# A gated linear-attention and mixture-of-experts kernel: the decayed k of the state update from untransposed k and a decay table that passes through DRAM

## The chip, the cores and the metric

The kernel runs on one core of one Trainium2 chip. The metric is device microseconds of one execution: the median of several. Engine names are those of the profile: PE (matrix engine; PEld its weight loads), DVE (vector), ACT (scalar), POOL, and SP, whose queue issues most DMAs.

## What is computed

```python
def _attn_ref(q, k, v, alpha):                    # (4, 8, 768, 48) each
    state = zeros((B, H, D, D))
    for t in range(S):
        state = alpha[:, :, t, :, None] * state + einsum('bhd,bhe->bhde', k[:, :, t], v[:, :, t])
        y[:, :, t] = einsum('bhd,bhde->bhe', q[:, :, t], state)

def _moe_ref(x, w_gate, w1, w2):                  # x (3072, 384), 8 experts, hidden 1024
    P = exp(logits - max);  8 rounds of row and column normalisation
    for e in range(E):
        out += P[:, e:e + 1] * (maximum(x @ w1[e], 0) @ w2[e])
```

The change touches the attention's state alone: over 128 tokens it is multiplied by the product of their alphas, and k^T v is added, each k times the alphas of the tokens behind it in these 128.

## The kernel before, in words

**Chunks and groups.** A batch element's 768 tokens are six chunks of 128. Two chunks make a group of 256 tokens, named batch_group: 0_0 to 3_2, twelve in all. The first four chunks (0_0 and 0_1) take a path of their own (`direct_chunk`) that the change leaves as it is. The other ten groups pass through `attn_block`, `attn_decays` and, for each chunk, `attn_chunk` with `attn_tail`.

**A group's block.** `attn_block` loads q, k and alpha with 16 tokens in a partition's row: 128 partitions are 16 sub-blocks of 8 heads. POOL and DVE multiply scores inside each 16 tokens (tile `AB`) and fold the alphas into q and k, so that `al[:, 0]` ends as the product of a sub-block's 16 alphas. The last step hands everything over through DRAM, all on SP's queue: `ks`, `qs`, `ds` (that product) and `As` are written and read back with tokens in the partitions as `KN`, `QN`, `DN`, `an`, and `VN` is loaded from v. The loads of the next block (`qt`, `al`, `kt`) stand behind it, on SP's queue or, for two groups, on POOL's.

**Decays.** `attn_decays` turns `DN` on PE (`psd`), and DVE and ACT build small tables from it (`pre`, `suf`, `q32`, `k32`, `q128`, `k128`, `dtot`): products of the sub-blocks' decays before or behind a sub-block.

**A chunk.** `attn_chunk` turns k and q on PE (`psk`, `psq`; copies `Tk`, `Tq`), makes decayed copies (`decq`, `deck`), multiplies scores (`psl`), and then multiplies `Tk` in place by `k128` on POOL. `attn_tail` computes y in `psy` from the old state `ST` and the scores `A`, turns the decayed k back with four PE transposes into `pskn`, copies it to `kb` on ACT, and multiplies `kb` with `VN` into `pss`, from which `ST` is updated. The last chunk of a batch element has no update: 16 of these 20 chunks turn k back. The chunk's y then goes, scaled, to `xT` (two f16 halves), the gate product `psg` reads it, and the experts read it later.

**What sets the order.** The two strings `START` and `UNIT` are an order written out by hand: `bN` is a step of block N, `cN` of chunk N, `dN` the decays of group N, `wN` a step of loading expert N's weights, `f` 0.45 us of expert matmuls (`moe_tile`; tiles `ps`, `h`, `r`). Each engine runs its instructions strictly in that order. The expert matmuls evacuate PSUM through four banks: in the first layer ACT writes the high half of `h` and DVE the low half, and a bank is free after DVE; in the second layer ACT alone copies to `r`. An expert's `w1` is loaded by eight DMAs into tile `xT` (`load_expert`), squared and summed by ACT (tile `w1m`), and PE multiplies the sums with `ones` into `pst_w`.

Of the kernel before, what the change touches and what calls it, by code (L numbers as in the profile page):

```python
# [9 lines left out]
F32 = mybir.dt.float32  # L10
# [15 lines left out]
def tile_gla_moe(ctx: ExitStack, tc: tile.TileContext, q, k, v, alpha, wg, w1, w2, out):  # L26
    nc = tc.nc
    B, H, S, D = q.shape
    NT, DM = out.shape
    E, _, FF = w1.shape  # L30
    P = 128
    U = 256
    NU = S // U
    NCH = U // P
# [3 lines left out]
    NP = H // 2  # L38
# [263 lines left out]
    for x in PRE + SUF + Q32 + K32:  # L302
        GE.memset(x, 1.0)

    ids = iter(range(1 << 20))
    hp1 = early.enter_context(tc.tile_pool(name="hp1", bufs=1, side="right"))
    fst = ExitStack()
# [24 lines left out]
    def load_v(x, b, t0, Q=SP):  # L332
        for r in range(2):
            Q.dma_start(x[:, :, r * DP:r * DP + D], v[b].rearrange("(j r) t d -> r t j d", r=2)[r, t0:t0 + P])
# [144 lines left out]
    def attn_block(b, u, got):  # L479

        g = b * NU + u
        t0 = u * U
        nm = f"{b}_{u}"
        vec = VE
        src = lambda x: x[b, :, t0:t0 + U].rearrange("h (n t) d -> n h (t d)", t=16)
        qt, kt, al = (ap1.tile([P, 16, D], F32, tag=x, name=f"{x}_{nm}") for x in ("qt", "kt", "al"))
        for x, y in ((qt, q), (al, alpha), (kt, k)):
            (GE if lop[0] else SP).dma_start(x, src(y))
        yield
        A = AB[g % 2]  # L490
        Af = A.rearrange("p s t -> p (s t)")
        pool = GE
        qd = qt

        def mult(eng, tag, shape, o, x, y):
            t = ap1.tile([P, *shape, D], F32, tag=tag, name=f"{tag}_{nm}_{next(ids)}")
            eng.tensor_mul(t, x, y)
            return o, t

        def total(o, t):  # L500
            vec.tensor_reduce(o, t, axis=AX.X, op=ALU.add)

        def level(L):

            nb = 8 // L
            Q = qd.rearrange("p (n z t) d -> p n z t d", z=2, t=L)
            K = kt.rearrange("p (n z t) d -> p n z t d", z=2, t=L)

            Dl = al.rearrange("p (n z t) d -> p n z t d", z=2, t=L)

            def cut(n, s, w):
                return ([w, L], A[:, n * 2 * L + s:n * 2 * L + s + w, n * 2 * L + L:(n + 1) * 2 * L],
                        Q[:, n, 1:2].to_broadcast([P, w, L, D]),
                        K[:, n, 0, s:s + w].unsqueeze(2).to_broadcast([P, w, L, D]))

            if L == 1:
                todo = [(pool, "tmp1", [8], Af[:, 1:256:34], Q[:, :, 1, 0], K[:, :, 0, 0])]
            elif L == 2:
                o = [bass.AP(tensor=Af.tensor, offset=Af.offset + s * 16 + 2, ap=[Af.ap[0], [68, 4], [1, 2]])
                     for s in range(2)]  # L520
                todo = [(pool, f"tmp{s + 1}", [4, 2], o[s], Q[:, :, 1],
                         K[:, :, 0, s:s + 1].to_broadcast([P, 4, 2, D])) for s in (1, 0)]
            elif L == 4:
                todo = [(pool, "tmp4", *cut(n, 0, 4)) for n in (1, 0)]
            else:
                todo = [(vec, "tmp8", *cut(0, 4, 4))] + [(pool, "tmp4", *cut(0, s, 2)) for s in (0, 2)]

            def merge(ko=kt, qo=qd):
                z = lambda x, i: x.rearrange("p (n z t) d -> p n z t d", z=2, t=L)[:, :, i]
                pool.tensor_mul(z(ko, 0), K[:, :, 0], Dl[:, :, 1, 0:1].to_broadcast([P, nb, L, D]))  # L530
                eng = pool if g in (2, 3) else vec
                eng.tensor_mul(z(qo, 1), Q[:, :, 1], Dl[:, :, 0, 0:1].to_broadcast([P, nb, L, D]))
                eng.tensor_mul(Dl[:, :, 0, 0], Dl[:, :, 0, 0], Dl[:, :, 1, 0])
            return todo, merge

        ko, qo = kt, qd
        if True:

            t = mult(pool, "tmp4", [16], Af[:, 0:256:17], qt, kt)
            yield  # L540
            total(*t)
            yield
            vec.tensor_mul(qt, qt, al)
            for L in (1, 2, 4, 8):
                todo, merge = level(L)
                for x in todo:
                    t = mult(pool if lop[0] else x[0], *x[1:])
                    yield
                    total(*t)
                    if L == 8:  # L550
                        yield
                merge()
            yield
        dma = SP.dma_start
        qs = dr.tile([H, U, D], F32, tag="qs", name=f"qs_{nm}")
        ks = dr.tile([H, U, D], F32, tag="ks", name=f"ks_{nm}")
        ds = dr.tile([H, 16, D], F32, tag="ds", name=f"ds_{nm}")
        As = dr.tile([H, U, 16], F32, tag="As", name=f"As_{nm}")
        qn, kn, dn = QN[g % 2], KN[g % 2], DN[g % 2]
        vn = VN[g % 2]  # L560
        an = ap2.tile([P, NCH, H, 16], F32, tag="an", name=f"an_{nm}")
        def put(t, t_):
            for x, y in ((ks, ko), (qs, qo)):
                dma(x[:, t:t_].rearrange("h (n t) d -> n h (t d)", t=16), y[t // 2:t_ // 2])

        put(0, U)
        dma(ds.rearrange("h n d -> n h d"), al[:, 0])
        if True:
            dma(As.rearrange("h (n s) t -> n h (s t)", s=16), Af)
        for c in range(NCH):  # L570
            sl = slice(c * P, (c + 1) * P)
            dma(kn[:, c, :, :D], ks[:, sl].rearrange("h t d -> t h d"))
            dma(qn[:, c, :, :D], qs[:, sl].rearrange("h t d -> t h d"))
            if c == 0:
                dma(dn[:, :, :D], ds.rearrange("h n d -> n h d"))
            dma(an[:, c], As[:, sl].rearrange("h p t -> p h t"))
            load_v(vn[:, c], b, t0 + c * P)
        got.update(qn=qn, kn=kn, dn=dn, vn=vn, an=an)
        yield

    def attn_decays(b, u, got):

        nm = f"{b}_{u}"
# [14 lines left out]
        e4 = ap2.tile([P, NCH, NP, 2], F32, tag="e4", name=f"e4_{nm}")  # L598
        dtot = ap2.tile([P, NCH, NP], F32, tag="dtot", name=f"dtot_{nm}")
        q128 = ap2.tile([P, NCH, NP, 2, 4], F32, tag="q128", name=f"q128_{nm}")  # L600
        k128 = ap2.tile([P, NCH, NP, 2, 4], F32, tag="k128", name=f"k128_{nm}")
        mul(x3(e2), d_[:, :, 0:4:2], d_[:, :, 1:4:2])
        cpy(x3(q32)[:, :, 1], d_[:, :, 2])
        cpy(x3(k32)[:, :, 0], d_[:, :, 1])
# [8 lines left out]
        cj = lambda x: x.rearrange("p c j z n -> p (c j) z n")  # L613
        e4b = lambda z: e4.rearrange("p c j z -> p (c j) z")[:, :, z:z + 1].to_broadcast([P, NCH * NP, 4])
        mul(cj(q128)[:, :, 1], cj(pre)[:, :, 1], e4b(0))
        mul(cj(k128)[:, :, 0], cj(suf)[:, :, 0], e4b(1))
        cpy(cj(q128)[:, :, 0], cj(pre)[:, :, 0])
        cpy(cj(k128)[:, :, 1], cj(suf)[:, :, 1])
        got.update(pre=pre, suf=suf, q32=q32, k32=k32, q128=q128, k128=k128, dtot=dtot)

    def attn_chunk(b, ch, got):

# [2 lines left out]
        first, last = ch == 0, ch == S // P - 1  # L625
        tt = b * (S // P) + ch
        nm = f"{b}_{ch}"
        T2 = []
        for s in "kq":
            ps = psa.tile([P, 512], F32, tag="psa", name=f"ps{s}_{nm}")  # L630
# [17 lines left out]
        def decayed_all(x, eng, tab):  # L648
            xi = x.rearrange("p j (n t) -> p (j n) t", t=16)
            eng.tensor_mul(xi, xi, tab.rearrange("p j z b -> p (j z b)").unsqueeze(2).to_broadcast([P, NP * 8, 16]))  # L650
# [30 lines left out]
        if not first:  # L681
            decayed_all(QT, VE, got["q128"][:, c])
        if not last:
            decayed_all(KT, GE, got["k128"][:, c])
        yield
        K_, Q_ = ([x[:, j] for j in range(NP)] for x in (KT, QT))
        yield from attn_tail(b, ch, vn[:, c], K_, Q_, A, got["dtot"][:, c])

    def attn_tail(b, ch, vn, KT, QT, A, dtot):

        first, last = ch == 0, ch == S // P - 1
        tt = b * (S // P) + ch
# [18 lines left out]
        y = psy[:, :DM]  # L711
        ab = ap2.tile([P, DM], BF16, tag="ab", bufs=1, name=f"ab_{nm}")
        SE.activation(ab, y, AF.Abs, scale=2.0 ** -10)
        if not last:
            psk = psa.tile([P, 512], F32, tag="psa", name=f"pskn_{nm}")
            for j in range(NP):
                tr(psk[:, j * P:(j + 1) * P], KT[j], ident)
            kb = ap2.tile([P, NP, P], F32, tag="kb", bufs=1, name=f"kb_{nm}")
            SE.copy(kb.rearrange("p j t -> p (j t)"), psk)
        yield  # L720
        psn = psy[:, DM:]
        for i in range(KT_):
# [10 lines left out]
        if not last:  # L733
            pss = psa.tile([P, 512], F32, tag="psa", name=f"pss_{nm}")
            for j in range(NP):
                for r in range(2):
                    pr = slice(r * DP, r * DP + D)
                    mm(pss[pr, j * D:(j + 1) * D], kb[:, j, pr], vn[:, j, pr])
            pv = pss[:, :NP * D].rearrange("p (j e) -> p j e", j=NP)
            for r in range(2):  # L740
                pr, cr = slice(r * DP, r * DP + D), slice(r * D, (r + 1) * D)
                if first:
                    SE.copy(Sn[pr, :, cr], pv[pr])
                else:
                    GE.tensor_mul(Sn[pr, :, cr], So[pr, :, cr],
                                         dtot[pr].unsqueeze(2).to_broadcast([D, NP, D]))
                    VE.tensor_add(Sn[pr, :, cr], Sn[pr, :, cr], pv[pr])
# [720 lines left out]
```

## Time and profile before

| | |
|---|---|
| median of 3 runs | 1655.09 us (1653.46 to 1657.01) |
| profiled execution, device time | 1656.76 us |
| its span, first to last instruction | 1655.1 us |
| PE busy | 1605.3 us, 97% |
| DVE, ACT, POOL busy | 1266.7, 933.0, 394.0 us |
| granted PE clock, mean | 0.987 of full |
| chain that ended last, PE's share | 86% |

The device time of the profiled execution is 1.7 us above its span. Rows of the trace give the start in us from the span's start, then the duration; `x16` behind a shape counts instructions merged into the row; brackets give the idle time before it and what ended it.

### The profile page before, as it was taken

How to read it: one execution, taken by the hardware profiler on the slowest of the kernel's cores; microseconds unless marked ns; L12 is line 12 of the kernel's file. 1: busy time of each engine (PE TensorE's matmuls, PEld its weight loads, DVE VectorE, ACT ScalarE, POOL GpSimd, SP SyncE). 2: the span in 40 equal slices, each digit the busy share in tenths (PEclk: the TensorE clock that was granted, in tenths of full speed). 3: DMA queues.
4: the chain of work that ended last, by engine and by line, in shares of the span. 5: the costliest groups of instructions: out<-in, count | busy, mean ns of one | idle time of the engine just before them, and what ended most of it. 6: DMA issues, size and time to landing. Idle time of an engine off the chain costs nothing.

```text
span 1655.1 us, 53978 instructions
## 1 busy us (share of the span) xinstructions
PE 1605.3 (97%) x23260; PEld 1429.1 (86%) x23260; DVE 1266.7 (77%) x2852; ACT 933.0 (56%) x2250; POOL 394.0 (24%) x395
## 2 busy tenths in 40 slices
PE   5689999999999999999999999999999999999998
PEld 4567777777777777777999999999999999999998
DVE  5877766665666574367798978898888888899998
ACT  4655543334333334355777767666766676666554
POOL 5447544643644462165000000000000000000000
PEclk9789999999999999999999999999999999999999
DMA  7463244144134313130312131213121312123332
GB/s 164 103 142 92 59 105 96 34 109 105 53 72 105 84 46 76 38 84 30 102 54 88 59 97 59 97 53 94 53 94 59 97 59 88 61 67 116 116 117 87
DMA packets 173903, 137.15 MB, mean 83 GB/s; under 512 B 109120, under 2 KB 163648, under 8 KB 173664
## 3 DMA queue, kind: packets, MB, share of 16 engines
q1 hardware_dynamic: 171920, 127.01, 28.0%
q0 software_dynamic: 1744, 6.70, 1.6%
q8 instruction: 182, 2.98, 0.7%
q14 instruction: 57, 0.47, 0.1%
HBM read 86.50 MB, written 47.17 MB: 81 GB/s over the span
## 4 chain that ended last, share of the span: by engine, by line
PE 86%; DVE 7%; ACT 3%; issue 2%; DMA 1%; SPq 0%; POOL 0%; DVEq 0%; ACTq 0%; POOLq 0%
PE ps L67 33%; PE p1a L67 13%; PE p2x L67 12%; PE p2y L67 6%; PE p1c L67 6%; PE p1d L67 4%; PE p2v L67 3%; PE psl L67 2%; PE psy L67 2%; DVE h L58 1%; DVE acc L58 1%; DVE hf L58 1%; DVE T L58 1%; ACT w L58 1%; DVE w L58 1%
## 5 line engine op out<-in xcount | busy, mean ns | idle before, releaser
L67 PEld LDWEIGHTS <-h 128*128 128x128 f16 x6684 | 570.3, 98 | 103.1 <-DVE h L58 0.8
L67 PEld LDWEIGHTS <-w 128*128 128x128 f16 x8424 | 602.3, 98 | 39.3 <-issue 6.6
L58 DVE TENSOR_TENSOR h<-hf,h 128x256 f16<-128x256 f32 x472 | 286.0, 616 | 34.3 <-ACT h L58 33.0
L67 PE MATMUL ps<-xT,w 128*128 128x256 f16 (+1 forms) x2664 | 302.3, 274 | 5.3 <-DVE h L58 3.2
L67 PE MATMUL ps<-w,h 128*128 128x384 f16 x1728 | 299.1, 327 | 0.2 <-DVE w L58 0.2
L67 PE MATMUL p2x<-w,h 128*128 128x192 f16 x2820 | 271.0, 246 | 0.0
L58 ACT CAST h<-hf 128x256 f16<-128x256 f32 x472 | 248.9, 570 | 13.1 <-DVE hf L58 8.2
L58 DVE TENSOR_TENSOR hf<-hf 128x256 f32<-128x256 f32 x354 | 181.6, 513 | 44.8 <-ACT hf L58 36.3
L58 DVE SCALAR_TENSOR_TENSOR h<-ps,h 128x256 f16<-128x256 f32 (+1 forms) x296 | 118.4, 413 | 115.3 <-ACT h L58 114.1
L58 ACT ACTIVATE h<-ps 128x256 f16<-128x256 f32 (+1 forms) x296 | 110.6, 376 | 161.7 <-PE ps L67 161.3
L58 POOL TENSOR_TENSOR tmp<-qt,kt 128x768 f32<-128x768 f32 (+2 forms) x87 | 156.8, 1808 | 133.9 <-DVE qt L58 84.3
L67 PE MATMUL p1a<-xT,w 128*128 128x128 f16 x2160 | 179.5, 219 | 0.0
L67 PE MATMUL p1c<-xT,w 128*128 128x128 f16 x2160 | 159.9, 219 | 0.0
L67 PEld LDWEIGHTS <-wx 128*128 128x128 f16 x2160 | 147.3, 98 | 7.2 <-issue 6.5
L58 ACT ACTIVATE hf<-p1d 128x256 f32<-128x256 f32 x118 | 45.1, 382 | 184.4 <-DVE h L58 157.7
L67 PE MATMUL p2y<-w,h 128*128 128x192 f16 x1404 | 135.0, 246 | 0.0
L67 PE MATMUL p1a<-xc,wx 128*128 128x128 f16 x1440 | 119.6, 219 | 4.7 <-ACT v L58 2.0
L58 DVE TENSOR_REDUCE AB<-tmp 128x16 f32<-128x768 f32 (+2 forms) x90 | 81.3, 903 | 53.0 <-POOL tmp L58 52.7
L58 ACT COPY r<-ps 128x384 f32<-128x384 f32 x72 | 34.2, 476 | 99.3 <-PE ps L67 60.2
L58 ACT COPY A<-psl 16x128 f32<-16x128 f32 (+3 forms) x164 | 52.4, 326 | 48.2 <-PE psl L67 46.6
L67 PE MATMUL p1d<-xT,wx 128*128 128x128 f16 x720 | 79.5, 219 | 0.0
L67 PE MATMUL p1a<-xc,w 128*128 128x128 f16 x720 | 79.5, 219 | 0.0
(237 smaller groups left out, 2020.3 us busy)
## 6 DMA issues: line engine op xcount, KB each, us to landing
accd<-acc SPq DMA_DIRECT2D x48, 384.0 KB, 2.6
acc<-accd SPq DMA_DIRECT2D x48, 384.0 KB, 3.2
raw<-r SPq DMA_DIRECT2D x72, 192.0 KB, 1.9
ri<-raw SPq DMA_DIRECT2D x72, 192.0 KB, 2.9
w1f<-in_moe_w_dram SPq DMA_DIRECT2D x20, 384.0 KB, 6.8
w2f<-in_moe_w_dram SPq DMA_DIRECT2D x5, 1536.0 KB, 6.9
VN<-in_v_dram SPq DMA_DIRECT2D x48, 96.0 KB, 2.9
out_dram<-acc SPq DMA_DIRECT2D x11, 384.0 KB, 4.0
```

What stands on the lines that cost most here:

```text
L58: r = f(*a, **k_)
L67: tc.keep_in_program_order(nc.tensor.matmul(out_, lhsT, rhs, start=start, stop=stop, **k_))
```

## The change

A second handover is added to the first. Every group's `al[:, 0]` is also written to a DRAM array `dsw` with 15 places for each head and chunk: eight are the chunk's sub-blocks, and the seven behind them hold ones, written once into each of two such arrays. Two DMAs read it as `win`: each partition is a sub-block and a head and gets the seven places behind its own. In `attn_decays` four DVE products reduce the seven to one decay (`win[:, 0]`), which goes to DRAM as `td` (16 sub-blocks by 384) and is read, sub-block by sub-block with 16 tokens each, as the tile `kb` at the start of `attn_chunk`. POOL multiplies `kb` by the untransposed `kn`, at the place where it multiplied `Tk`. The four transposes, the `pskn` bank, the ACT copy and the table `k128` go; `kb` has two buffers in place of one. `win` shares the buffer `tmp2` of the block.

```diff
+    dsw = [dr.tile([H, NCH, 15, D], F32, tag=f"dsw{i}", bufs=1, name=f"dsw{i}") for i in range(2)]
...
     def attn_block(b, u, got):
...
+        if g < ND // NCH + 2:
+            SP.dma_start(dsw[g % 2][:, :, 8:].rearrange("h c n d -> (h c) n d"),
+                         ones[:2 * H, None, :D].to_broadcast([2 * H, 7, D]))
...
         dma(ds.rearrange("h n d -> n h d"), al[:, 0])
+        for c in range(NCH):
+            dma(dsw[g % 2][:, c, :8].rearrange("h n d -> n h d"), al[c * 64:c * 64 + 64, 0])
...
             load_v(vn[:, c], b, t0 + c * P)
+        win = ap1.tile([P, 7, D], F32, tag="tmp2", name=f"win_{nm}")
+        for c in range(NCH):
+            e = dsw[g % 2][0, c, 1]
+            dma(win[c * 64:c * 64 + 64], bass.AP(tensor=e.tensor, offset=e.offset,
+                                                 ap=[[D, 8], [NCH * 15 * D, H], [1, 7 * D]]))
...
     def attn_decays(b, u, got):
...
         mul(cj(q128)[:, :, 1], cj(pre)[:, :, 1], e4b(0))
-        mul(cj(k128)[:, :, 0], cj(suf)[:, :, 0], e4b(1))
         cpy(cj(q128)[:, :, 0], cj(pre)[:, :, 0])
-        cpy(cj(k128)[:, :, 1], cj(suf)[:, :, 1])
+        win = got["win"]
+        mul(win[:, 0:3], win[:, 0:3], win[:, 3:6])
+        mul(win[:, 0], win[:, 0], win[:, 6])
+        mul(win[:, 1], win[:, 1], win[:, 2])
+        mul(win[:, 0], win[:, 0], win[:, 1])
+        td = dr.tile([NCH * 8, DM], F32, tag="td", name=f"td_{nm}")
+        SP.dma_start(td.rearrange("n (h d) -> n h d", h=H), win[:, 0])
+        tab = []
+        for c in range(NCH):
+            e = td[c * 8]
+            tab.append(bass.AP(tensor=e.tensor, offset=e.offset, ap=[[DM, 8], [0, 16], [1, DM]]))
...
     def attn_chunk(b, ch, got):
...
+        kb = None
+        if not last:
+            kb = ap2.tile([P, H, D], F32, tag="kb", name=f"kb_{nm}")
+            SP.dma_start(kb, got["tab"][c])
...
         if not last:
-            decayed_all(KT, GE, got["k128"][:, c])
+            GE.tensor_mul(kb, got["kn"][:, c, :, :D], kb)
...
-        if not last:
+        if not last and kb is None:
             psk = psa.tile([P, 512], F32, tag="psa", name=f"pskn_{nm}")
             for j in range(NP):
                 tr(psk[:, j * P:(j + 1) * P], KT[j], ident)
-            kb = ap2.tile([P, NP, P], F32, tag="kb", bufs=1, name=f"kb_{nm}")
-            SE.copy(kb.rearrange("p j t -> p (j t)"), psk)
+            kb = ap2.tile([P, H, D], F32, tag="kb", name=f"kb_{nm}")
+            SE.copy(kb, psk.rearrange("p (h d) -> p h d", h=H)[:, :, :D])
```

SP's queue in group 0_2, the first that goes through `attn_block`; `xT` are the weights of expert 2. Before:

```order
L58 DMA an_2_1939<-As_2_1938 128x8x16
L58 DMA VN_123<-in_v_dram 128x4x48 x2
L58 DMA KN_118<-ks_2_1936 128x8x48
L58 DMA QN_116<-qs_2_1935 128x8x48
L58 DMA an_2_1939<-As_2_1938 128x8x16
L58 DMA VN_123<-in_v_dram 128x4x48 x2
L58 DMA xT_1_80<-in_moe_w_dram 32x3x512 x4
L58 DMA xT_1_83<-in_moe_w_dram 32x3x512 x4
L58 DMA xT_2_81<-in_moe_w_dram 128x4x384
```

The same place after:

```order
L58 DMA KN_118<-ks_2_1939 128x8x48
L58 DMA QN_116<-qs_2_1938 128x8x48
L58 DMA an_2_1942<-As_2_1941 128x8x16
L58 DMA VN_123<-in_v_dram 128x4x48 x2
L58 DMA win_2_1960<-dsw_148 64x1x336 x2
L58 DMA dsw_149<-ones 16x7x48
L58 DMA td_2_2000<-win_2_1960 128x48
L58 DMA kb_4_2003<-td_2_2000 128x1x384
L58 DMA xT_1_80<-in_moe_w_dram 32x3x512 x4
L58 DMA xT_1_83<-in_moe_w_dram 32x3x512 x4
```

Five DMAs now stand between the last `VN` load and the weights, among them `td`, which reads what DVE has written, and `kb`, which reads what `td` has written.

DVE's queue at the decays of group 1_2, as in all later groups; `xT` here is the low half of a chunk's output, which `psg` on PE reads. Before:

```order
L58 TENSOR_TENSOR dtot_2_4609<-e_1_2_4608 128x8
L58 TENSOR_TENSOR q_1_2_4610<-pre_130,e_1_2_4608 128x8x4
L58 TENSOR_TENSOR k_1_2_4611<-suf_132,e_1_2_4608 128x8x4
L58 TENSOR_TENSOR xT_1_83<-ys_3_4538,xT_1_80 128x3x128
L58 TENSOR_TENSOR decq_1_4_4671<-Tq_4_4669,q_1_134 128x256
L58 TENSOR_TENSOR deck_1_4_4673<-Tk_4_4662,k_1_136 128x256
```

The same place after:

```order
L58 TENSOR_TENSOR dtot_2_4617<-e_1_2_4616 128x8
L58 TENSOR_TENSOR q_1_2_4618<-pre_130,e_1_2_4616 128x8x4
L58 TENSOR_TENSOR win_2_4599<-win_2_4599 128x144
L58 TENSOR_TENSOR win_2_4599<-win_2_4599 128x48 x3
L58 TENSOR_TENSOR xT_1_83<-ys_3_4541,xT_1_80 128x3x128
L58 TENSOR_TENSOR decq_1_4_4684<-Tq_4_4682,q_1_134 128x256
```

The one table product is replaced by the four products on `win`, whose first needs both `win` DMAs landed. On PE the 16 rows of four transposes into `pskn` are gone and nothing else has moved; on POOL each product on `Tk` is replaced in place by one on `kb`.

## Rows read from the trace of the kernel before

**Rows 1.** Windows: length; busy PE, PEld, DVE, ACT, POOL; clock; DMA share; GB/s.

```profile
120.00:160.00 40.00, 37.68 (x474) 28.59 (x473) 30.09 (x59) 23.70 (x54) 26.29 (x22) 1.00 0.33 93
200.00:300.00 100.00, 99.79 (x1309) 76.45 (x1308) 68.70 (x132) 38.85 (x109) 46.85 (x39) 1.00 0.38 91
```

**Rows 2.** The tile `pskn`: duration min/median/max ns, first and last start.

```profile
L70 PE MATMUL pskn<-ident,Tk x64: 272/273/330, 145.7 to 679.5; 128*128 128x128 f32 x64
```

**Rows 3.** Timeline of PE: the transposes of one chunk and what follows.

```profile
223.22 0.66 PE L70 MATMUL pskn<-ident,Tk 128*128 128x128 f32 x4
223.72 2.11 PE L67 MATMUL ps<-w,h 128*128 128x384 f16 x12
```

**Rows 4.** The chain that ended last, in group 0_2.

```profile
113.01 4.32 DMA VN<-in_v_dram
...
117.80 6.60 DMA xT<-in_moe_w_dram
...
124.91 3.40 ACT w L58 x8
...
128.36 0.39 PE pst_w L67 x2
```

**Rows 5.** Timeline of SP's queue in group 0_2.

```profile
112.26 1.20 SPq L58 DMA_DIRECT2D VN<-in_v_dram  x2
113.51 14.62 SPq L58 DMA_DIRECT2D xT<-in_moe_w_dram  x10
```

**Rows 6.** Timeline of DVE in group 0_2: the table product.

```profile
114.57 0.19 DVE L58 TENSOR_TENSOR k<-suf,e 128x32 f32<-128x32 f32 x1
```

**Rows 7.** The tile `ds`: writing and reading 24 KB, 20 DMAs.

```profile
DMA to landing us min/median/max: 2.1/3.4/5.0
```

**Rows 8.** Windows of 4 us around group 0_2.

```profile
104.00:108.00 4.00, 2.04 (x131) 1.74 (x127) 3.11 (x13) 0.68 (x3) 0.17 (x1) 0.97 1.09 280
...
116.00:120.00 4.00, 4.00 (x69) 3.18 (x68) 3.27 (x4) 1.19 (x3) 3.23 (x3) 0.75 1.03 212
```

**Rows 9.** Timeline of DVE in group 1_0.

```profile
169.55 0.19 DVE L58 TENSOR_TENSOR k<-suf,e 128x32 f32<-128x32 f32 x1
170.78 0.52 DVE L58 TENSOR_TENSOR decq<-Tq,q 128x256 f32<-128x256 f32 x1 [1.04 <-ACT Tq L58]
171.22 2.11 DVE L58 TENSOR_TENSOR deck<-Tk,k 128x256 f32<-128x256 f32 x1
173.26 2.02 DVE L58 TENSOR_TENSOR decq<-Tq,pre 128x256 f32<-128x256 f32 x1
...
177.87 0.74 DVE L58 SCALAR_TENSOR_TENSOR h<-ps,h 128x256 f16<-128x256 f32 x2
```

**Rows 10.** Timeline of POOL beside it.

```profile
170.97 2.08 POOL L58 TENSOR_TENSOR A<-an,mask 128x1024 f32<-128x1024 f32 x1
```

**Rows 11.** Timeline of DVE, the next chunk's `deck`.

```profile
188.03 0.84 DVE L58 TENSOR_TENSOR deck<-Tk,k 128x256 f32<-128x256 f32 x1
```

**Rows 12.** Timeline of SP's queue in group 1_0.

```profile
167.18 5.29 SPq L58 DMA_DIRECT2D VN<-in_v_dram  x2
```

**Rows 13.** Timeline of PE in group 1_0: first-layer matmuls, nine a bank.

```profile
173.48 2.13 PE L67 MATMUL ps<-xT,w 128*128 128x256 f16 x18
...
177.21 3.12 PE L67 MATMUL ps<-xT,w 128*128 128x256 f16 x27
```

**Rows 14.** Timeline of DVE in group 1_2.

```profile
286.25 0.18 DVE L58 TENSOR_TENSOR k<-suf,e 128x32 f32<-128x32 f32 x1
286.92 0.56 DVE L58 TENSOR_TENSOR xT<-ys,xT 128x384 f16<-128x384 f32 x1 [0.49 <-ACT xT L58]
290.70 0.51 DVE L58 TENSOR_TENSOR decq<-Tq,q 128x256 f32<-128x256 f32 x1 [3.22 <-ACT Tq L58]
```

**Rows 15.** Timeline of PE in group 1_2: the gate product.

```profile
290.81 0.29 PE L67 MATMUL psg<-wg,xT 128*128 128x18 f16 x6
```

**Rows 16.** Timeline of SP's queue in group 1_2.

```profile
283.30 1.38 SPq L58 DMA_DIRECT2D VN<-in_v_dram  x2
```

More of the change, by code (lines that the diff above doesn't have):

```diff
@@ L577, in attn_block @@
             load_v(vn[:, c], b, t0 + c * P)
+        win = ap1.tile([P, 7, D], F32, tag="tmp2", name=f"win_{nm}")
[3 more added lines that the diff above has]
+                                                 ap=[[D, 8], [NCH * 15 * D, H], [1, 7 * D]]))
+        got["win"] = win
         got.update(qn=qn, kn=kn, dn=dn, vn=vn, an=an)
@@ L600, in attn_decays @@
         q128 = ap2.tile([P, NCH, NP, 2, 4], F32, tag="q128", name=f"q128_{nm}")
-        k128 = ap2.tile([P, NCH, NP, 2, 4], F32, tag="k128", name=f"k128_{nm}")
         mul(x3(e2), d_[:, :, 0:4:2], d_[:, :, 1:4:2])
@@ L615, in attn_decays @@
         mul(cj(q128)[:, :, 1], cj(pre)[:, :, 1], e4b(0))
-        mul(cj(k128)[:, :, 0], cj(suf)[:, :, 0], e4b(1))
         cpy(cj(q128)[:, :, 0], cj(pre)[:, :, 0])
-        cpy(cj(k128)[:, :, 1], cj(suf)[:, :, 1])
-        got.update(pre=pre, suf=suf, q32=q32, k32=k32, q128=q128, k128=k128, dtot=dtot)
+        win = got["win"]
[9 more added lines that the diff above has]
+            tab.append(bass.AP(tensor=e.tensor, offset=e.offset, ap=[[DM, 8], [0, 16], [1, DM]]))
+        got.update(pre=pre, suf=suf, q32=q32, k32=k32, q128=q128, tab=tab, dtot=dtot)
     def attn_chunk(b, ch, got):
@@ L683, in attn_chunk, with attn_tail @@
         if not last:
-            decayed_all(KT, GE, got["k128"][:, c])
+            GE.tensor_mul(kb, got["kn"][:, c, :, :D], kb)
         yield
         K_, Q_ = ([x[:, j] for j in range(NP)] for x in (KT, QT))
-        yield from attn_tail(b, ch, vn[:, c], K_, Q_, A, got["dtot"][:, c])
-    def attn_tail(b, ch, vn, KT, QT, A, dtot):
+        yield from attn_tail(b, ch, vn[:, c], K_, Q_, A, got["dtot"][:, c], kb)
+    def attn_tail(b, ch, vn, KT, QT, A, dtot, kb=None):
         first, last = ch == 0, ch == S // P - 1
@@ L737, in attn_tail @@
                     pr = slice(r * DP, r * DP + D)
-                    mm(pss[pr, j * D:(j + 1) * D], kb[:, j, pr], vn[:, j, pr])
+                    mm(pss[pr, j * D:(j + 1) * D], kb[:, 2 * j + r, :D], vn[:, j, pr])
             pv = pss[:, :NP * D].rearrange("p (j e) -> p j e", j=NP)
```

## The prediction

> **What bounds the kernel now.** I read the busy time by stage first. The reader is to see PE there: 99.79 us busy of 100 from 200 to 300 us, 37.68 of 40 from 120 to 160 [rows 1]. Once the expert matmuls run without a break PE is the bound, so a PE instruction taken out there is time won in full, and a stall put in there is time lost in full. Then the view of the tile `pskn`: 64 transposes, the first at 145.7 us, the last at 679.5, all in that stretch [rows 2]. Last, the chain that ended last, because the first group of the new path runs before PE is saturated: in group 0_2 it goes through a `VN` load that lands at 113.01 + 4.32 = 117.33, a weight load `xT` that lands at 117.80 + 6.60 = 124.40, ACT's squares of these weights, and `pst_w` on PE at 128.36 [rows 4]. So SP's queue at 113.5 is on the path that sets the end, and that is where the change puts five more DMAs.
>
> **What it removes.** The price of a transpose is not its duration of 273 ns, since matmuls overlap. It is the step from the start of the four to the start of the next matmul: 223.72 - 223.22 = 0.50 us [rows 3]; the two other chunks that I read gave 0.49. 16 chunks x 0.495 = **7.9 us won**. The ACT copy and the table product `k128` that go too are worth nothing: they lie beside a saturated PE and PE does not wait for them. POOL's product on `kb` stands where the one on `Tk` stood, with 384 columns in place of 512; nothing either. The `pss` matmuls keep their shape.
>
> **What it adds, group 0_2.** SP ends the last `VN` issue at 113.46 (112.26 + 1.20) and began the weights at 113.51 [rows 5]. Now two `win` DMAs come between. They queue behind `VN`, which lands at 117.33 [rows 4], and bring 172 KB: I take 118.5, with 117.3 and 119.5 as ends. DVE, which did the table product at 114.57 [rows 6], waits for them; its four products, each hardly more than the 0.19 of that one and in part dependent, take about 0.8 (estimate), to 119.3. `td` waits for DVE and `kb` for the landing of `td`; two such transfers are in the rows of `ds`, 2.1 to 5.0 us, median 3.4 [rows 7]. I take 2.4, near the lowest, because the queue is empty then: 121.7. With 0.6 for the issue of `kb` the weights start at 122.3, not at 113.51. Before, the eighth weight load landed 10.9 us after the first issue, behind a full queue. Now eight issues at 0.6 (`VN` took 1.20 for two) and one landing of 3.4 give 8.2: 130.5 in place of 124.40. ACT's four squares took 3.40 [rows 4]; two of them can run while the other four loads land, so 1.75 are left: 132.3, against 128.31. PE waits at `pst_w` **4.0 us longer**. Ends: 1.6 (`win` together with `VN`, 2.1 for `td`, loads in 7.4) and 8.4 (119.5, 5.0, 9.1). DVE's own delay here ends before that and is covered by the same wait of PE.
>
> **PE's clock in that wait.** From 104 to 108 PE was busy 2.04 of 4 us; from 116 to 120, busy throughout, its mean granted clock was still 0.75 [rows 8]: it had fallen from 2.4 to 1.2 GHz in between and came back in that slice, which cost 1.0 us of it. A wait of five us at 128 is a deeper hole than that of 104. I take 1.0 to 2.0, **1.5 us lost**; ends 0 (the clock stays) and 5 (ten us at half clock).
>
> **Group 1_0.** SP ends the last `VN` issue at 172.47 (167.18 + 5.29) [rows 12]: the `win` issues, 0.6 each, end at 173.6 and land at about 176.1 (2.5 after). DVE wanted to pass at 169.55 and began `decq` at 170.78 [rows 9]. Now it begins at 176.9, 6.1 late. It gets some of this back: `deck` and the second `decq` took 2.11 and 2.02 beside POOL's `A` and what follows it on POOL [rows 9, 10], but 0.84 [rows 11] and 0.52 [rows 9] without; POOL is done before 176.9, so 2.8 come back and the low half of `h` is 3.3 late. PE needs it: the five first-layer tiles start at 173.48 (two) and 177.21 (three, 1.0 apart) [rows 13], there are four banks, and the fifth, at 179.25, takes the bank that DVE freed at 178.25 (177.87 and one product) [rows 9]. 3.3 late against a slack of 1.0: **2.4 us lost**. Ends: 1.5 (`win` in 2.1 after the first issue) and 6.0 (nothing regained, landing in 3.4).
>
> The Trainium skill ("SBUF — State Buffer", section "SBUF: two separate sides") says that VectorE and GpSimd share one port pair by an exclusive lock, held for the whole instruction, so that the other one waits. Rows 9 to 11 agree with it: 2.11 beside a POOL instruction of 2.08, 0.84 without. By it the delayed DVE work runs free of POOL; if contention followed it instead, this group would lose 2.8 more and the kernel come out at 1659.2.
>
> **The other eight groups.** In 1_2 SP ends `VN` at 284.68 [rows 16]; the two `dsw` issues push that by about 0.5 (most of their 1.2 falls into waits for landings), the second `win` starts at 285.8 and lands at 288.8 (3.0, between 2.1 and 3.4 [rows 7]). DVE is there at 286.25, but it idles anyway before `decq` at 290.70, for 3.22 us [rows 14]. The products end at 289.6, `xT` 0.56 later at 290.2, and `psg` reads it at 290.81 [rows 15]: covered, by 0.6. That cover is gone if the landing takes 3.6; at 4.3, as `VN` in group 0_2 [rows 4], 0.7 a group is lost. I take 0 for most, 1.0 for the seven groups 1_2 to 3_2 together (ends 0 and 10), and 0.3 for 1_1, which lies between them and 1_0 (ends 0 and 2.4). Behind DVE's wait stand `xT` and `decq`, then the low halves of `h`; behind SP's wait for `td` stand the `raw` stores of expert results, whose two buffers `r` are wanted again only some us later, and `kb`, which POOL wants more than ten us after the decays. The loads of the next block start up to 2.4 later and DMA is idle after them. All nothing.
>
> **Sum.** -7.9 + 4.0 + 1.5 + 2.4 + 0.3 + 1.0 = **+1.3 us**. The profiled execution took 1656.76 us, 1.7 above its span and 1.7 above the median 1655.09; the sum on it gives 1658.1, and on the median **1656.4 us**. About 0.2%, 3.3 us, is what a measurement of this kernel can tell from no change: the forecast is none.
>
> **Rivals.**
> (A) The handover hides. For it: the weights need only land before ACT reaches them, DMA is empty while SP waits, and the first half is squared while the second lands. Against: `td` and `kb` are two round trips in series with the chain. At the low ends: -7.9 + 1.6 + 1.5 = -4.8, **1650.3 us**, faster.
> (B) The hole at `pst_w` costs the clock as well as the wait. For it: 104 to 120 [rows 8], where the clock fell after PE was half idle. Against: PE has unbroken work behind `pst_w`. It decides from a wait of some six us on, that is with `td` at the median 3.4 and a `win` at 119.5: 6.5 for the wait, 4 for the clock, the rest as above: -7.9 + 6.5 + 4 + 2.4 + 0.3 + 1.0 = +6.3, **1661.4 us**, slower.
> The Trainium skill ("TensorE: Matmul & The Clock Gate", section "What's actually happening") calls the throttled clock the default that activity releases; by that an idle hole at 128 does turn it down and unbroken work gives it back, which is the 1.5 of the sum rather than the 4 of this rival. The trace agrees at 116 to 120.
> (C) DVE's wait is exposed in the seven later groups, because `win` lands late behind a crowded queue. For it: 4.32 for `VN` in 0_2 [rows 4]. Against: the idle 3.22 us. From a landing of 3.6 on; at 4.6, 1.0 a group: -7.9 + 4.0 + 1.5 + 2.4 + 0.3 + 7 = +7.3, **1662.4 us**.
> (D) PE does not gain the 0.495 per chunk because something else is late there. Against: PE has no wait in these stretches. -7.9 becomes -4: 1660.3.
>
> **How the numbers follow.** Forecast (between -3.3 and +3.3) 0.47; A 0.20; B 0.18; C 0.10; D and mixtures on the slow side 0.05. Faster by over 0.2% is A, 0.20; slower is B, C and D, 0.33. The range runs from 1649.5, just below A, to 1664.5, above C and a worse B; it leaves out ends that would have to come together.
>
> **What would show it.** In the profile after: no `pskn` but for the first four chunks and the same matmul following `psy` directly; DVE idle before the first `win` product, near 4 us in 0_2, 6.5 in 1_0, 2 to 3 later; the weight loads of expert 2 issued near 122; `pst_w` near 132 and a low clock behind it; one wait of PE for `h` of some 2 us in 1_0; none for `psg` later. It is wrong if PE waits after 200 us, if the weights land before 127, or if the stretch from 200 to 700 us is not shorter by about 7 us.

## The result, and the profile after

| | before | after |
|---|---|---|
| median | 1655.74 us (1653.46 to 1657.01, 4 runs) | 1668.07 us (1665.41 to 1669.27, 4 runs) |
| profiled execution: device time, span | 1656.76, 1655.1 us | 1669.27, 1667.2 us |
| granted PE clock, mean | 0.987 | 0.984 |

The ratio is 1.0074 (95% interval 1.0056 to 1.0092): slower, by 12.3 us. The forecast was 1656.4 us, no change, with a range up to 1664.5. The forecast of no change was wrong, and the time lies above the range.

Who made PE wait between 120 and 720 us, after (us in total, times, longest; the three rows that differ from before):

```profile
PE pst_w L67 <- ACT w L58: 8.1, 1, 8.1
PE ps L67 <- DVE h L58: 4.7, 3, 2.4
PE psg L67 <- DVE xT L58: 3.0, 4, 1.1
```

The same view before has 0.9 for `pst_w`, 0.7 for `psg` (one wait, at 126 us, which both kernels have) and none for `h`. The waits after stand in PE's timeline, each with its length in brackets; the four `pss` rows are used below as marks, because the same `pss` matmuls start at 122.63, 152.31, 218.99 and 682.78 before.

```profile
122.61 0.56 PE L67 MATMUL pss<-VN,kb 128*48 128x48 f32 x16 [1.05 <-DVE lg L58]
...
135.46 0.59 PE L67 MATMUL pst_w<-w1m,ones 128*128 128x4 f32 x2 [8.05 <-ACT w L58]
...
162.08 0.56 PE L67 MATMUL pss<-VN,kb 128*48 128x48 f32 x16
...
191.50 1.14 PE L67 MATMUL ps<-xT,w 128*128 128x256 f16 x9 [2.39 <-DVE h L58]
...
222.59 3.26 PE L67 MATMUL ps<-w,h 128*128 128x384 f16 x19 [0.69 <-DVE h L58]
...
233.17 0.56 PE L67 MATMUL pss<-VN,kb 128*48 128x48 f32 x16
...
253.53 2.12 PE L67 MATMUL ps<-xT,w 128*128 128x256 f16 x18 [1.66 <-DVE h L58]
...
308.29 0.28 PE L67 MATMUL psg<-wg,xT 128*128 128x8 f16 x5 [0.64 <-DVE xT L58]
...
366.84 0.28 PE L67 MATMUL psg<-wg,xT 128*128 128x8 f16 x5 [1.11 <-DVE xT L58]
...
424.75 0.28 PE L67 MATMUL psg<-wg,xT 128*128 128x8 f16 x5 [0.51 <-DVE xT L58]
...
694.99 0.56 PE L67 MATMUL pss<-VN,kb 128*48 128x48 f32 x16
```

The granted clock behind the two longest waits, in windows of 4 us (length; busy PE, PEld, DVE, ACT, POOL; clock; DMA share; GB/s):

```profile
128.00:132.00 4.00, 0.00 (x0) 0.00 (x0) 0.12 (x2) 1.76 (x4) 3.84 (x5) 0.96 1.08 201
132.00:136.00 4.00, 0.54 (x3) 0.54 (x4) 0.00 (x0) 1.76 (x4) 0.61 (x1) 0.50 1.01 330
136.00:140.00 4.00, 4.00 (x14) 1.83 (x13) 2.71 (x8) 2.90 (x5) 0.00 (x0) 0.50 0.03 11
140.00:144.00 4.00, 4.00 (x21) 2.23 (x20) 2.33 (x4) 0.96 (x3) 2.44 (x2) 0.76 0.14 49
188.00:192.00 4.00, 1.61 (x16) 1.29 (x14) 4.00 (x8) 3.21 (x5) 1.72 (x1) 1.00 0.39 110
192.00:196.00 4.00, 4.00 (x126) 3.32 (x125) 3.70 (x10) 2.25 (x6) 3.13 (x3) 0.64 0.27 97
196.00:200.00 4.00, 4.00 (x33) 3.25 (x32) 3.97 (x7) 2.30 (x8) 4.00 (x4) 0.93 0.00 0
```

Before, the windows from 128 to 164 and from 184 to 200 all have 1.00. By these clocks a window of 4 us at 0.50 loses 2.0 us of PE's work, one at 0.64 loses 1.4.

With the marks the whole difference can be booked. Up to 122.61 the two kernels are level (-0.02). Then:

| between the marks | before | after | longer | waits of PE | transposes gone | rest: the clock, where it fell |
|---|---|---|---|---|---|---|
| 122.6 to 162.1 | 29.68 | 39.47 | 9.79 | 8.05 - 0.93 = 7.12 | 1 x -0.48 | 3.15 |
| 162.1 to 233.2 | 66.68 | 71.09 | 4.41 | 2.39 + 0.69 | 1 x -0.48 | 1.81 |
| 233.2 to 695.0 | 463.79 | 461.82 | -1.97 | 1.66 + 0.64 + 1.11 + 0.51 | 14 x -0.48 | 0.83 (clock 1.00) |

The sum is 12.2 us, and behind the last mark nothing more is lost (972.3 and 972.2 us to the end). The 0.83 of the last row is no clock: taken chunk by chunk, each of its four waits costs some 0.16 more than its bracket says, and 0.31 lies between the marks around `psg` at 540.89, whose six matmuls take 0.60 where the other sixes take 0.29 or 0.30; `xT` on DVE, which they read, took 2.28 there (538.87) and not 0.55. The -0.48 a chunk is read where PE does not wait: from one chunk's `pss` to the next, in group 2_1, it takes 9.90 us before (448.03 to 457.93) and 9.42 after (463.39 to 472.81).

**The chain in group 0_2**, which answers to [rows 4], and SP's queue there, which answers to [rows 5]:

```profile
115.36 3.24 DMA win<-dsw
...
119.64 1.48 DMA td<-win
...
125.44 8.14 DMA xT<-in_moe_w_dram
...
133.65 1.77 ACT w L58 x4
...
135.46 0.59 PE pst_w L67 x2
```

```profile
114.69 1.28 SPq L58 DMA_DIRECT2D win<-dsw  x2
...
119.64 0.35 SPq L58 DMA_DIRECT2D td<-win  x1
121.13 0.59 SPq L58 DMA_DIRECT2D kb<-td  x1
122.17 5.95 SPq L58 DMA_DIRECT2D xT<-in_moe_w_dram  x10
```

The landing of `win` (118.60) and the first weight load (122.17) are where the prediction had them (118.5 and 122.3). Between them `td` landed sooner than forecast, in 1.48 for 2.4, and the other steps took longer, so the second agreement is partly chance. Then the last of the eight loads takes 8.14 us to land.

**DVE in groups 1_0 and 1_2**, which answers to [rows 9] and [rows 14], and POOL in 1_2:

```profile
186.54 0.91 DVE L58 TENSOR_TENSOR win<-win 128x144 f32<-128x144 f32 x4 [7.13 <-DMA win<-dsw]
...
191.03 0.75 DVE L58 SCALAR_TENSOR_TENSOR h<-ps,h 128x256 f16<-128x256 f32 x2
...
304.82 2.95 DVE L58 TENSOR_TENSOR win<-win 128x144 f32<-128x144 f32 x4 [3.93 <-DMA win<-dsw]
307.68 0.55 DVE L58 TENSOR_TENSOR xT<-ys,xT 128x384 f16<-128x384 f32 x1
```

```profile
305.57 1.89 POOL L58 TENSOR_TENSOR A<-an,mask 128x1024 f32<-128x1024 f32 x1
```

DVE waits for `win` in every one of the ten groups. The four products take 0.91 us alone and 2.95 beside POOL. In 2_0, with the longest of the three later waits at `psg`, they are not slow: `win` is issued at 360.08 and 360.71, and DVE has it at 365.40.

```profile
365.40 0.91 DVE L58 TENSOR_TENSOR win<-win 128x144 f32<-128x144 f32 x4 [6.00 <-DMA win<-dsw]
```

### The profile page after: what moved, and what is told of

It reads as the page before. It is cut to its first block, busy times and chain, and to the rows that moved or that the text cites. A ratio compares the mean times of both kernels' runs of the same rounds, so it can differ in the third digit from the quotient of the medians.

```text
span 1667.2 us, 53940 instructions
## 1 busy us (share of the span) xinstructions
PE 1603.6 (96%) x23196; PEld 1425.0 (85%) x23196; DVE 1255.8 (75%) x2882; ACT 923.9 (55%) x2224; POOL 389.7 (23%) x395
## 4 chain that ended last, share of the span: by engine, by line
PE 82%; DVE 8%; SPq 4%; DMA 2%; ACT 2%; issue 2%; POOL 0%; DVEq 0%; ACTq 0%; POOLq 0%
PE ps L67 28%; PE p1a L67 14%; PE p2x L67 13%; PE p2y L67 7%; PE p1c L67 7%; PE p1d L67 5%; SPq L58 4%; PE p2v L67 3%; PE psl L67 2%; PE psy L67 2%; DMA win<-dsw 1%; DVE h L58 1%; DVE T L58 1%; ACT w L58 1%; DVE acc L58 1%
## 5 line engine op out<-in xcount | busy, mean ns | idle before, releaser
L67 PEld LDWEIGHTS <-w 128*128 128x128 f16 x8424 | 602.7, 99 | 44.8 <-issue 12.3
L67 PE MATMUL p1d<-xT,w 128*128 128x128 f16 x720 | 79.4, 219 | 0.0
```

The lines of the kernel that those rows point to most:

```text
L67: tc.keep_in_program_order(nc.tensor.matmul(out_, lhsT, rhs, start=start, stop=stop, **k_))
```

## The experiments

The profiled executions differ by some us in where the first 120 us end (the mark of 122.61 after stands at 125.38 in one run below, at 119.65 in another), so stretches are measured from that mark.

**The gain alone.** All of the handover is left out, with its products; `kb` is `k` times one.

```diff
-        win = ap1.tile(...); its loads, dsw, td, the loads of kb, the products on win
-            GE.tensor_mul(kb, got["kn"][:, c, :, :D], kb)
+            GE.tensor_mul(kb, got["kn"][:, c, :, :D], ones[:, None, :D].to_broadcast([P, H, D]))
```

> The changed kernel with the whole handover left out: no dsw, win, td, no load of kb, no products on win; POOL multiplies the untransposed k by ones into kb. It leaves out the decay of k in the state update. It keeps the removal of the transposes, of the ACT copy and of the table k128. Theory (the transposes give back 0.495 us a chunk, and all of the loss comes from the handover): 1655.7 - 7.9 = about 1647.8 us, ratio to before 0.9952, no wait of PE at pst_w above 1 us and none after 130. Rival D (PE does not gain the transposes in full): 1651.7 us.

Measured: 1647.47 us (1645.97 to 1648.84), ratio 0.9944 (0.9929 to 0.9958). The gain is there, and rival D falls. From the first mark to the last it takes 553.30 us, 6.85 less than before: the 7.7 of the transposes less a new wait of 0.70 and a little behind it. PE's timeline shows the old wait at `pst_w`, and one that neither part of the sum had:

```profile
127.32 0.39 PE L67 MATMUL pst_w<-w1m,ones 128*128 128x4 f32 x2 [0.94 <-ACT w L58]
...
207.28 2.94 PE L67 MATMUL ps<-w,h 128*128 128x384 f16 x17 [0.70 <-DVE h L58]
```

So the 0.69 at 222.59 after is no cost of the handover. It belongs to the removal: here, as after, DVE's product `tmp` of 1536 elements takes 3.36 us where it took 1.75 before, and `h` stands behind it. The rows show why. Before, POOL's product on `Tk` waited for `psl` on PE; the one on `kb` does not, so POOL is done with it earlier and its own `tmp` falls on DVE's. In the run below that keeps the transposes (the handover alone) DVE's `tmp` takes 1.75, and this wait is not there. DVE, before and after:

```profile
202.02 1.75 DVE L58 TENSOR_TENSOR tmp<-qt,kt 128x1536 f32<-128x1536 f32 x1
```

```profile
216.51 3.36 DVE L58 TENSOR_TENSOR tmp<-qt,kt 128x1536 f32<-128x1536 f32 x1
```

POOL, before and after:

```profile
204.92 1.06 POOL L58 TENSOR_TENSOR Tk<-Tk,k 128x512 f32<-128x512 f32 x1 [3.53 <-PE psl L67]
```

```profile
216.44 1.82 POOL L58 TENSOR_TENSOR tmp<-qt,kt 128x768 f32<-128x768 f32 x1
```

**The loads of `win` earlier**, behind the first chunk's loads of a group.

```diff
             load_v(vn[:, c], b, t0 + c * P)
+            if c == 0:
+                (the tile win and its two loads)
-        (the tile win and its two loads)
```

> The changed kernel with one move: the two loads of win stand behind the first chunk's loads of a group, not behind the second chunk's. Theory (DVE's wait for win delays h, and with it PE, in 1_0 and 1_1, and xT for psg later; the clock falls in the wait of 1_0): DVE's wait is gone, and with it 2.4 + 1.7 us in 1_0, 2.3 in 1_1, 2.3 of psg; in 0_2 the weights start near 118.7 instead of 122.2, 3.5 less wait: 1668.1 - 12.2 = about 1656 us. Rival (DVE is late there for another reason, beside POOL): DVE's idle time is gone, but PE still waits for h and psg: about 1664 us.

Measured: 1657.74 us (1655.73 to 1660.06), ratio 1.0010 (0.9999 to 1.0021). Of the 12.3 us lost, 10.3 come back. In 0_2 the weights start at 116.26 and the wait at `pst_w` is 3.25; in 1_0 PE has no wait but the removal's 0.70, and the clock stays at 1.00; the waits at `psg` after 130 us are gone. A wait of 0.63 for `h` is left in 1_1. But PE now also waits for `h` in 1_2, 2_0 and 2_1 (2.38, 0.81, 0.97), which I had not expected. In 1_2 this goes back to POOL, which waits for the `kt` of the next block:

```profile
299.29 1.80 POOL L58 TENSOR_TENSOR tmp<-qt,kt 128x768 f32<-128x768 f32 x1 [4.54 <-DMA kt<-in_k_dram]
```

DVE's `AB` sum waits for this product and `h` stands behind it on DVE. On SP the loads of the next block come last, behind the group's handover and the added one: they are pushed back by whatever goes ahead of them.

**In 0_2, the weights ahead of `td` and `kb`.**

```diff
-        SP.dma_start(td.rearrange(...), win[:, 0])        # in group 0_2 not here
-            SP.dma_start(kb, got["tab"][c])               # nor here
...
         yield
+        if tt == 4:
+            got["td"]()
+            SP.dma_start(kb, got["tab"][c])
         psl = ...
```

> The changed kernel with one move: in group 0_2 alone, td and the load of kb are issued behind the weight loads of expert 2; win stays. Theory (the wait at pst_w follows the start of the weight loads, and the low clock behind it follows the wait): the loads start near 117, 5.3 us earlier; the wait at pst_w falls from 8.1 to about 2.8 us and the clock stays up: 1668.1 - 5.3 - 3.2 = about 1659.6 us. Rival 1 (the wait goes but the clock falls all the same): 1662.8. Rival 2 (the loads land by what DMA is doing otherwise, not by their start): the wait stays near 8, 1668.

Measured: 1659.88 us (1655.46 to 1663.00), ratio 1.0018 (1.0006 to 1.0030), the time that the theory gave; rival 2 falls. The wait at `pst_w` is 2.14 us in the profiled run. The theory's clock is not met: it still fell, as rival 1 had it, though for a shorter time, which costs 1.5 us in the first window below and not 3.2. The first stretch (123.57 to 155.66) is 7.4 us shorter than after, where the theory gave 8.5; the rest of the saving lies behind it, so that the median meets 1659.6 is partly chance.

```profile
132.00:136.00 4.00, 4.00 (x17) 2.01 (x16) 3.09 (x4) 3.73 (x5) 0.62 (x1) 0.63 0.18 67
136.00:140.00 4.00, 4.00 (x35) 3.21 (x33) 1.71 (x4) 1.25 (x3) 0.00 (x0) 1.00 0.25 85
```

**Both moves.** The edits are the two above, and both fills of ones are issued in the first block.

```diff
-        if g < ND // NCH + 2:
-            SP.dma_start(dsw[g % 2][:, :, 8:]..., ones...)
+        if g == ND // NCH:
+            for x in dsw:
+                SP.dma_start(x[:, :, 8:]..., ones...)
```

> Both moves (win behind the first chunk's loads; in group 0_2 td and kb behind the weight loads), and the two fills of ones issued at the start of the first block of this path. Theory (losses of the two are separate): what is left is some 2.4 us in 0_2, where the win loads still stand ahead of the weights: 1655.7 - 7.9 + 2.4 = about 1650.2 us, ratio to before 0.9967, faster than both kernels. Rival (the extra DMAs themselves slow the others, wherever they stand): 1655 or more.

> The kernel of both moves once more, as the comparison for e9 on the same chip. Theory and rival: 1652.7 us, ratio to before 0.9974, as in its first runs.

Measured: 1652.67 us (1650.93 to 1655.21), ratio 0.9974 (0.9964 to 0.9985); again, 1653.74 us, ratio 0.9984 (0.9973 to 0.9995). It beats both kernels, though by less than the theory's 1650.2. Moves of DMA issues alone turn a loss of 12.3 us into a gain of some 3. In the first profile the wait at `pst_w` is 1.24 us and the clock behind it 1.00; what is left is 1.78 for `DN` in 1_0 and 0.70, 0.45 and 0.55 for `h`.

```profile
126.89 0.39 PE L67 MATMUL pst_w<-w1m,ones 128*128 128x4 f32 x2 [1.24 <-ACT w L58]
```

```profile
128.00:132.00 4.00, 4.00 (x26) 2.39 (x25) 2.90 (x5) 3.68 (x5) 1.82 (x2) 1.00 0.45 168
```

**PE kept busy in the wait.**

```diff
             ps = psa.tile([P, 512], F32, tag="psa", name=f"pst_{nm}_{e}")
+            if (e, nm) == (2, "w1"):
+                for _ in range(34):
+                    mm(ps.rearrange(...), onesb, ones.bitcast(BF16)...)
             mm(ps[:, :4], ones, ss)
```

> The changed kernel with 34 dummy matmuls of 128x512 on PE ahead of the expert-2 pst_w matmul: PE is busy (34 x 0.213 = 7.2 us) where it waited, and nothing comes earlier or later by them. Theory (the wait at pst_w costs its own 7.1 us and the lower clock behind it about 3.2 more): the wait for ACT stays, the clock is 1.00 from 136 to 144 us and 3 us come back: about 1665 us. Rival (the slow stretch behind the wait is due to something else, such as late h): unchanged, 1668 us.

Measured: 1664.22 us (1663.21 to 1665.74), ratio 1.0047 (1.0032 to 1.0062), some 4 us less than after, for adding work.

```profile
136.00:140.00 4.00, 4.00 (x26) 2.43 (x25) 2.87 (x6) 3.48 (x5) 0.00 (x0) 1.00 0.01 2
140.00:144.00 4.00, 4.00 (x38) 3.51 (x36) 2.83 (x6) 1.93 (x5) 3.01 (x3) 1.00 0.29 102
```

From mark to mark (122.39 to 158.56) it takes 36.17 us against 39.47 after: 3.30, about the 3.15 that the table books to the clock. `pst_w` itself stands as far behind the first mark as after (12.80 and 12.85 us), so nearly all of it lies behind the wait. The clock is a cost of its own. The Trainium skill ("TensorE: Matmul & The Clock Gate", section "What's actually happening") says that activity is what releases the throttle. The dummy matmuls, whose results nobody uses, agree.

**The handover alone**, added to the kernel before and not used, with the transposes kept.

```diff
+ dsw, its writes, win, the four products, td, as in the change
+            ku = ap2.tile([P, H, D], F32, tag="ku", bufs=1, name=f"ku_{nm}")
+            SP.dma_start(ku, got["tab"][c])
```

> The kernel before with the handover added and not used: dsw, win, the products, td and the loads of the table (into a buffer of its own, one of it for want of room) all run, but the transposes into pskn, the ACT copy and k128 stay. Theory (gain and loss add up): 1668.1 + 7.9 = about 1676 us. Rival (part of the loss exists only because PE has less to do): 1672 us or less.

Measured: 1671.40 us (1670.77 to 1676.64), ratio 1.0096 (1.0076 to 1.0117). I expected 1676; the median is the rival's, that gain and loss don't simply add, though one of the four runs took 1676.64. PE's waits from 120 to 720 us:

```profile
PE pst_w L67 <- ACT w L58: 6.9, 1, 6.9
PE ps L67 <- DVE h L58: 3.0, 2, 2.6
PE psg L67 <- DVE xT L58: 1.9, 3, 0.7
```

From the mark at 120.55 to the last one (697.01) it takes 576.46 us, 16.3 more than before. After loses 12.2 there and the gain alone wins 6.85, so its handover costs 19.1. The 2.8 us between the two lie behind the mark in 1_0 (233.17 after): 4.8 us against 2.0; ahead of it the differences cancel. There PE's waits are 3.9 us after and 1.6 here. That PE, with more of its own to do, comes later to what DVE owes it would explain this, but it is argued from one profile of each and not shown. The difference in `pst_w` (6.9 against 8.1) is between two runs and I don't ascribe it.

**The two large loads of `w2` later**, behind the first `raw` stores.

```diff
-                    (GE if lop[0] else SP).dma_start(x..., src...)
+                    if e == 2:
+                        held.append((x..., src...))
...
         yield
+        if tt == 4:
+            for x in held:
+                SP.dma_start(*x)
         psl = ...
```

> The changed kernel with the two 768 KB loads of expert 2's w2 issued behind the first two raw stores instead of straight behind the eight w1 loads. Theory (the eight loads, 1.57 MB, land at the rate that DMA moves, some 205 GB/s, and the w2 loads take part of that): the last w1 load lands about 2.5 us earlier, near 131; PE's wait at pst_w falls from 8.1 to about 5.6: about 1665 us. Rival (each load has a fixed time to landing whatever is beside it): the last w1 load stays at 133.6 and the time at 1668 us.

Measured: 1666.58 us (1664.79 to 1668.21), ratio 1.0060 (1.0044 to 1.0076): 1.5 us less than after, inside the noise of the two ratios. The landings tell more. ACT squares the first four loads and then the last four; the second wait ends when the last has landed. After:

```profile
133.65 0.84 ACT L58 ACTIVATE w<-xT 128x768 f16<-128x768 f32 x1 [2.10 <-DMA xT<-in_moe_w_dram]
```

With `w2` later, where the loads start at 124.49:

```profile
135.02 0.84 ACT L58 ACTIVATE w<-xT 128x768 f16<-128x768 f32 x1 [0.67 <-DMA xT<-in_moe_w_dram]
```

The last one has landed 10.5 us after the first issue, against 11.5 after; PE waits 6.65, against 8.05. So about 1 us of the landing is due to `w2`, not the 2.5 that I expected. The load of `kb` ahead of the eight may weigh about as much: in the weights-first run, where it stands behind them, the last has landed 10.7 us after the first issue (118.01 to 128.70). Most of it is the eight loads themselves. With `w2` later SP issues nothing else behind the load of `kb`, and from 128 to 132 us DMA is full:

```profile
128.00:132.00 4.00, 1.46 (x21) 0.97 (x19) 2.86 (x7) 0.00 (x0) 2.23 (x2) 1.00 1.03 223
```

At these 223 GB/s the eight loads of 192 KB, 1.57 MB in all, take 7.1 us (an estimate).

**The queue of the added DMAs.** In the kernel of both moves, from 1_0 on, `dsw` and `win` go to POOL's DMA queue.

```diff
-            dma(dsw[g % 2][:, c, :8]..., al...)
+            (GE if g > 2 else SP).dma_start(dsw[g % 2][:, c, :8]..., al...)
...
+                    (GE if g > 2 else SP).dma_start(win[z * 64:z * 64 + 64], ...)
```

> The kernel of both moves (e4), but from group 1_0 on the dsw writes and win loads are issued on POOL's DMA queue, at the end of the block, and not on SP's. Theory (what is left of the loss in e4 is that these four issues push DN and the next block's loads back on SP's queue): PE's wait for DN at 167 and the waits for h in 1_2 and 2_1 go, 1652.7 - 3 = about 1649.5 us. Rival (POOL's queue now waits for the dsw landings, and deck, A and the next block's loads stand behind it): slower than e4, 1655 us or more.

Measured: 1653.59 us (1651.75 to 1656.53), ratio 0.9983 (0.9974 to 0.9993), no better than both moves on SP. From 300 to 700 us PE is now busy 400.00 us of 400, so the theory holds there. But in 1_1 PE waits 2.89 us for `h`, by the mechanism of the rival, if not at its price of 1655 or more: the next block's loads stand on POOL's queue behind `win`, which waits for `dsw`, and POOL then waits for `kt`.

```profile
235.14 1.81 POOL L58 TENSOR_TENSOR tmp<-qt,kt 128x768 f32<-128x768 f32 x1 [7.50 <-DMA kt<-in_k_dram]
```

```profile
240.00:244.00 4.00, 2.41 (x64) 2.02 (x64) 3.93 (x9) 0.64 (x2) 2.15 (x3) 1.00 0.00 0
244.00:248.00 4.00, 4.00 (x110) 3.43 (x106) 4.00 (x7) 3.12 (x11) 3.92 (x4) 1.00 0.02 4
```

In 0_2, behind a wait of 1.86 us at `pst_w`, the same run shows a low clock:

```profile
128.00:132.00 4.00, 4.00 (x17) 1.99 (x16) 3.28 (x5) 3.53 (x5) 0.69 (x1) 0.62 0.25 90
```

**Each group its queue:** SP's in 0_2 and 1_1, POOL's in 1_0 and from 1_2 on, by which of the two traces had the smaller waits there.

```diff
-            (GE if g > 2 else SP).dma_start(...)
+            (SP if g in (2, 4) else GE).dma_start(...)
```

> The kernel of both moves with the queue of dsw and win chosen by group: on SP's queue (win behind the first chunk's loads) in 0_2 and 1_1, on POOL's queue in 1_0 and from 1_2 on. Theory (each group keeps the queue on which the loads of the next block were not late in the traces of e4 and e8): the waits for DN (1.8) and for h in 1_2 and 2_1 (1.0) of e4 and the 2.9 of e8 in 1_1 are gone: about 1650.5 us, 2 less than e4. Rival (other waits take their place, by what is next late): as e4, 1652.7 us.

Measured: 1651.28 us (1649.32 to 1652.37), ratio 0.9966 (0.9954 to 0.9978), against 0.9984 (0.9973 to 0.9995) for both moves, measured beside it. It lies between the theory's 1650.5 and the rival's 1652.7. It is the fastest version that keeps the reference's computation. Its interval meets that of the SP version, so that it beats that one is likely and not shown. Its waits are 1.17 at `pst_w`, 1.35 for `h` in 1_0, 0.70 and 0.67 after that, none from 1_2 on, where the SP version beside it had 1.91, 1.39 and 0.98. The rival is right in part: the SP version beside it had no such wait in 1_0.

## Why the prediction was wrong

**The gain, -7.9: right.** 16 x 0.48 = 7.7, and the run without the handover gives it. What was missed is a wait of 0.7 that the removal itself brings back. The step that missed it is that POOL's product on `kb` changes "nothing either": it no longer waits 3.53 us for `psl`, and what follows it on POOL meets DVE.

**Group 0_2, +4.0: the place was right, the size wrong.** It is 7.1. The start of the weights was met (122.17 for 122.3). The step that failed is "eight issues at 0.6 and one landing of 3.4", together 8.2: the eight issues took 3.6 us, and the last landing came 7.8 behind them. I took the landing from DMAs of 24 KB [rows 7] and set aside 6.60, for this very load [rows 4], as the work of a full queue. The queue was empty this time, and the eight loads took 11.4 from the first issue to the last landing, more than the 10.9 of before. Most of that is their 1.57 MB, which no empty queue makes smaller; at the 223 GB/s of the run with `w2` later it is 7.1 us (an estimate). The correction of ACT's squares (1.75 left) was right.

**The clock, +1.5: mis-sized.** It is 3.15 in 0_2, and 1.8 more in 1_0 where the sum had none. Rival B had this cost but let it begin at a wait of six us; 0.63 and 0.62 stand behind waits of 2.14 and 1.86 us in 0_2 (the weights-first run and the POOL-queue run). Rival B's own sum has a slip: 1.0 more for `win` and 1.0 more for `td` make a wait of 6.0, not 6.5, and 1660.9 us.

**Group 1_0, +2.4: right** in place and mechanism, and in size (2.39) partly by luck. DVE was held until 186.54 and ran its delayed work free of POOL, 0.42 for each of `decq` and `deck`. `decq` came 6.8 us late and not 6.1, but DVE won back 3.4 and not 2.8. In the runs with the same code in this group, the wait is 1.05 (weights first), 0.94 (PE kept busy) and 2.80 (`w2` later).

**Group 1_1, +0.3, and the seven later ones, +1.0: mis-sized.** They are 1.66 (DVE had waited 6.55 us for `win`) and 2.3, with what the table leaves over about 3. "Covered, by 0.6" had three errors. `VN` ends on SP 2 us later in 1_2 than before (301.22, where 284.68 [rows 16] plus the 14.55 by which this stretch is late gives 299.23); I had 0.5, since I took most of the `dsw` issues to fall into waits. The products were priced at 0.8 wherever they run, while in 1_2 and 2_1 they met POOL's `A` and took 2.95 and 3.04. And in 2_0 DVE had `win` 4.7 us after the second issue, which is the case of rival C (4.6, 1.0 a group; the wait was 1.11). In 1_2 and 2_1 one product took 1.93, about the 1.89 of `A`. The Trainium skill ("SBUF — State Buffer", section "SBUF: two separate sides") tells of a lock that VectorE and GpSimd hold for a whole instruction, and the trace agrees. The prediction priced this for 1_0 and forgot it here, where it would have given rival C a larger chance.

**"All nothing" for the next block's loads: wrong as a general statement.** After the change it did no harm that can be told from the rest, but the runs with `win` earlier and with POOL's queue show 2.4 to 2.9 us of PE's time lost through a late `kt`.

**The signs that were named.** Right: DVE idle for 3.79 us in 0_2 and 7.13 in 1_0, weights at 122, one wait for `h` of 2 us in 1_0, a low clock behind `pst_w`. Wrong: `pst_w` near 132 (135.46), DVE idle for 2 to 3 us in the later groups (1.32 to 6.55), no `psg` wait later (three), and a stretch from 200 to 700 us shorter by 7 us (from mark to mark it is 2 shorter). Rival A, that the handover hides, fell with the first wait; it hid in none of the first six groups.

**The range.** It left out "ends that would have to come together". Several did come together: transfers landed later than the row that was used for them (the weights in 0_2, `win` in 2_0), and SP's queue handed the delay of the `dsw` issues on. Rivals A to D were priced one at a time; B and C together, with the 7.1, give -7.9 + 7.1 + 4 + 2.4 + 0.3 + 7 = +12.9, 1668. That this meets the measured time is luck: the 7 of rival C was about 3, and the rest came from the clock in 1_0, from 1_1 and from the removal's own wait.

## What to carry to other kernels

A gain on a saturated engine is easy to read and to trust; the price of a DMA round trip is what stands behind it on its queue, so first look for a place in that queue where nobody waits behind it. Price a load by the row of that load (10.9 us from first issue to last landing here, before; 11.4 after), or by its bytes over the rate in the windows, and not by a small transfer's landing. Where several terms depend on the same queue, add their bad ends together.

## What the runs showed of the hardware

Waits of PE of 1.86 to 2.39 us in 0_2 and 1_0 were followed by a granted clock of 0.62 to 0.64 in the next window of 4 us, and one of 2.38 in 1_2 by 0.59 (the run with `win` earlier). Waits of 2.89 and 1.66 in 1_1 (the POOL-queue run and after) and of 1.91 in 1_2 (both moves, again) were followed by 1.00. So the length of the wait alone does not decide it; what does stays open here.

The eight weight loads, 192 KB to 32 partitions each, moved at some 220 GB/s with all DMA engines busy (223 and a share of 1.03 from 128 to 132 us, with `w2` later); from 132 to 136 us after, where the two `w2` loads of 768 KB to 128 partitions take over, DMA shows 330 GB/s. Whether the partitions or the size of a load make the difference was not tested.
